# Two state-space convolutions, gated: Dskip added out of PSUM, the spilled tile stored and loaded by units, one tile for a chunk's last sum, u spectra stored in pairs, a new order of work

## The chip, the cores and the metric

The kernel runs on one core of a Trainium2 chip. A core has five engines, each with its own queue, which it works off in order: TensorE (PE in the profile; PEld is its loading of weights), VectorE (DVE), ScalarE (ACT), GpSimd (POOL) and SyncE (SP). SP here only issues transfers; 16 DMA engines carry them out. TensorE writes its sums to PSUM, the other tiles lie in SBUF. The metric is the device time of one execution in microseconds (us). Lower is better. The number given for the kernel is the median of three runs.

## The reference, cut to what matters

There are two parameter sets, A and B, over the same input u, with L = 2048 positions, D = 512 channels and N = 128 states. Each set makes a causal convolution kernel K for every channel out of 128 decaying, turning exponentials, convolves u with it by a Fourier transform of twice the length, and adds u times Dskip. A gate per position mixes the two results.

```python
def ref(u, A_re, A_im, B_re, B_im, C_re, C_im, log_dt, Dskip):
    dt = jnp.exp(log_dt)[:, None]
    logdA, dB = dt * (A_re + 1j * A_im), dt * (B_re + 1j * B_im)
    P = jnp.exp(logdA[:, :, None] * jnp.arange(L)[None, None, :])
    K = jnp.einsum("dn,dnl,dn->dl", C_re + 1j * C_im, P, dB).real
    Kf, Uf = rfft(pad(K, L)), rfft(pad(u.T, L))
    return irfft(Uf * Kf)[:, :L].T + u * Dskip

g = sigmoid((u * gate_w).sum(-1, keepdims=True))
out = g * ref(u, *A) + (1 - g) * ref(u, *B)
```

All data are float32. Adding Dskip to K at position 0 is the same as adding u times Dskip, and that is how both versions of the kernel do it.

## The kernel before, in words

The 512 channels are worked in NCH = 8 chunks of 64; with the two parameter sets a chunk has CH = 128 rows. A chunk is made of 8 tiles of 16 rows, 64 tiles T in all.

- `tables(T)` makes the exponentials of a tile as products of small tables. GpSimd makes angles (`ang`) and magnitudes (`mr`, "any": GpSimd or VectorE), ScalarE takes two sines and a square (L284), VectorE multiplies (`ei` and `mr`, L271 and L281). `kgen` (L588) sums over the 128 states on TensorE into a PSUM bank `c` and leaves the 16 rows of K. A copy of 256 columns (on ScalarE, L294, or VectorE, L296) brings them to half of an SBUF tile `kt` (L592). After each second tile VectorE adds Dskip (`dsk`) to column 0 of the eight groups in `kt` (L594), and `first` (L606) does the first step of the Fourier transform into `xa` or `xb`, the chunks in turn.
- `u_spectra` does the same for u, once for each pair of chunks b. Its eight spectra (L620) go from PSUM through a tile `z` to DRAM (`us`), 256 KB each. `gated` (L650) computes the gate into `gsi`, and loads its input through tiles `f`.
- `conv(c, j)` loads a spectrum of u back (`u<-us`), makes the spectrum of K (L620) and multiplies the two on VectorE (`y`, L684). After each second j, `back(c, U)` runs the first step of the inverse transform for unit U of four (`inv`, L704, 128 matmuls). Its two halves x are copied to a tile `z` each, and each is stored to the spilled tile `zb` of the chunk in DRAM, 256 KB (L712). In DRAM the half's four groups are rows 16x + 4U of 32; each row of `zb` has 136 x 128 places, of which 128 x 128 are used.
- `fin(cs, k)` does the last sum, for a quarter k of the positions. It loads 4 KB for each of 128 partitions from `zb` (512 KB a chunk, `f<-zb`), runs 32 matmuls (L740) with the gated weights `gsi`, copies the result to `o` and stores it. The chunks are taken in the groups FINS: three pairs, where one matmul spans two chunks (128 columns), then chunk 6 and chunk 7 alone (64 columns). A quarter needs all four units of its chunks. Chunk 7's four quarters are loaded in four pieces each: 192 KB, 192 KB, 64 KB and 64 KB, into tiles `ei` and `mr` that are free by then.

The order of all this is written out by hand. The body of `ssm_mix` calls the pieces one after the other, and `Plan` numbers each operation (0 to 1874) and notes which tiles it reads and writes. ORDER is a list of these numbers in the order in which they are emitted. So it sets the order within each engine's queue; a "b" behind a number takes the second of the engines that the operation allows (for a copy VectorE in place of ScalarE, for an "any" product VectorE in place of GpSimd, for a late store GpSimd's queue in place of SP's). `Plan.order` hands out the buffers of a ring (`z` 3, `f` 2, `o` 2, PSUM `c` 4) in that order, and an operation that takes a buffer waits for the users of the one before. All other transfers are issued by SP, in order: a transfer at the head of SP's queue that waits for its data holds up those behind it.

Of the kernel before, what the change touches and what calls it, by code (L numbers as in the profile page):

```python
# [34 lines left out]
FINS = ((0, 1), (2, 3), (4, 5), (6,), (7,))  # L35
# [11 lines left out]
def constants():  # L47
# [16 lines left out]
    si = np.stack([np.cos(ang).T, -np.sin(ang).T], 1).reshape(2 * G1, NB)  # L64
# [19 lines left out]
8 10 11 9 12 7 6 2 4 0 1 186 3 83 182 5 82 491 85 87 367 84 86 18 19 20 21 22 23 25 26 27 28 29 30 24 31 32 33 34 17 88 35 37  # L84
38 36 39 40 45 44 41 42 46 47 48 49 51 50 183 73 74 52 53 75 184 382 76 43 79 54 56 55 57 185b 58 187 61 189 62 188 138 67 59
60 63 64 65 68 69 70 71 72 369 66 77 370 371 78 372 81 384 383 80 385 91 92 93 94 95 190 194 342 96 16 13 98 99 101 100 191
102 104 89 373 103 105 192b 90b 376 195 374 375 377 401 107 196 106 193 386 378 379 108 109 402 380 197 387 388 15 14 127 219
# [3 lines left out]
133 131 445 199 425 368 437 438 439 440 441 208 448 226 212 200 1419 209 1430 449 446 426 447b 427 442 450 451 141 148 452  # L91
462 474 476 475 477 464 497 429 465 428 466 149 144 453 142 143 151 454 145 146 150 139 455 492 467 495 152 154 468 153 494
156 155 469 140 157 456 493 496 470 498 501 147 502 159 471 158 160 472 503 499 517 478 479 480 481 482 161 162 483 457 484
473 165 166 171 506 485 172 173 164 486 487 163 167 507 508 458 174 168 169 459 460b 175 500 177 179 504 625 628 627 626 629
170 505 488 518 515 516 532 533 534 344 490b 489b 509 510 1423 1420 1431 176 624 180 511 1424 1421 512 1432 1425 519 345 520
# [3 lines left out]
1446 559 1453 574 353 598 575 599 1447 1448 607 609 608 610 585 586 1454 601 354 1438 602 587 588b 355 589 560 1450 600 611  # L99
562 612 603 604 633 1466 613 761 649 356 561b 614 615 616 630 631 634 605 617 606b 650 357 1456 618 1457 635 636 637 619b 638  # L100
590 223 639 592 224 640 620 647 648 641 642 591b 225b 651 643 652 665 667 666 1440 1449 1451 234 227 621 653 229 228 644 623b
655 656 654 622 669 1458 1459 230 757 235 657 1461b 658 231 670 236b 237b 1463 1460 1474 1462 262 266 233b 232b 645 671 256
678 668 679 695 358 257 247 659 250 672 673 674 248b 675 680 696 681 682 646 251 683 660 359 363 685 686 241 253 1475 676 258
249 242 254 697 684 677 700 252 1771 255 243 661 361 365 698 1467 709 699 360 710 364 711 244 259 701 245 260 238 1464 687
1468 1476 688 239b 1465 689 703 690b 662 664b 704 691 1478 760 758 702 762 663 705 706 246 1485 1477 261 1469 1486 1776 240
1479 1487 707 712 726 728 727 366 362 713 1472 714 1470 708 716 717 715 692 739 729 740 718 719 1499 1488 1480 693 694 741
1481 730 1489 742 1490 720 1518 1471 766 1482 1473 1496 731 721 722 1500 723 1483 732 733 734 763 767 743 764 724 725 744
1491 735 1501 736 1497 1494b 1492b 737 747 1498 738b 263 267 265b 748 745 893 759 746 264 269 1484 1510 1493 1507 270 1502
769 768 780 765 770 781 771 749 750 268b 1503b 1505b 774 772 751 752 773 753 775 782 783 797 271 754 272 273 776 755b 756 799
784 785 777 800 787 274 1495 1504 1506 302 889 798 275 801 778 788 779b 277 276 786 284 1519 278 299 802 803 789 285b 790  # L110
1520 805 1777 1772 286 891 300 279 804 1511 1508 290 806 1512 1509 807 1773 791 811 812 813 291 815 1774b 808 1529 306 280
1521 1778 828 814 830 829 831 818 816 792 819 1779 817 296 297 843 832 281 1775 301 1781 292 809 833 810 282 820 793 821 841
835 822 293 287 283 842 844 836 834 823 824 845 874 859 837 838 1532 1782 294 846 847 848 892 890 894 794 288b 796b 795b 839
849 850 851 852 840b 1522 1513 860 861 872 873 862 875 1523 1530 853 295 1786 289 1514b 1516b 1531 854b 855 1787 1515 825 863
864 856 865 826 827 858 895 899 896 900 866 867 868 857b 869 876 877 879 1533 1524 1788 1534 880 878 1525 1789 901 298 1780
1540 1783 1527 904 870 905 881 1784b 871b 1544 1535 898 1543 1526 902 882 1545 1528 1551 883 1541 1025 906 1026 1023 1024 913
915 897 916 903 914 932 930 933 931 1536b 884b 1538b 1542 907 303 307 304 308 908 305b 309b 909 917 1562 1537 314 1539 1554
315 918 317 316b 910 885 1546 1547 919 920 886 921 1549b 943 887 888 934 911 922 923 944 963 310 311 1555 912 935 312 936 313
937 938 1517 1548 1552 924 318 1556 1553 948 949 945 319 925b 939 946 1563 330 336 327 940 1564 961 1030 962 964 947 1785
1550 1790 1796 320 1022 1791 1027 926 951 952 941 337 950 328 942 338 329 965 324 333 339 953 331b 332 954 325b 966 955 321  # L120
326 1565 967 956 334 340 993 322 968 969 976 974 977 975 970 927 978 929 979 957 971 991 994 992 972 928b 981 982 958 980 973
959 996 960 997 983 995 1007 1005 1008 1006 335 341 1576 1031 1573 984 999 1566 1557 1560 998 1558 1577 985 1574 1000 1567
1009 986 1010 1001 1012 1002 1568 323 1559 1575 1578 1013 1569b 1587 1584 1585 1003 1561 1570 1598 1156 1571 1011 1157 1004
1579 1588 1028 1034 1029 1032 1033 1045 1046 1035 1065 1014 1586 1015 1582b 1036 1016 1580 1037 1017 1047 1038 1606 1572 1581
1589 1590 1039 1040 987 1018 1048 1063 1049 1066 1064 1041 988 1050 1591 1593 1051 1042 1053 1052 990 989 1019 1043 1054 1592
# [76 lines left out]
def ssm_mix(ctx: ExitStack, tc: tile.TileContext, a, out, dry=False):  # L202
# [39 lines left out]
    if not dry:  # L242
# [13 lines left out]
        for b in range(NCH // 2):  # L256
            for j in range(NJ):
                tiles["uspec", b, j] = dp.tile([2, 128, 4 * DC], F32, name=f"us{b}_{j}")
# [575 lines left out]
```

## Time and profile before

| | us |
|---|---|
| median of 3 runs | 494.34 |
| lowest and highest | 491.32, 497.35 |
| the profiled execution, whole time | 495.32 |
| its span in the profile | 493.6 |

| transfer in the profile | count | KB each |
|---|---|---|
| zb<-z (store of half a unit) | 64 | 256 |
| f<-zb (load of a quarter) | 28 | 512 |
| mr<-zb, ei<-zb (chunk 7) | 8 and 8 | 192 and 64 |
| us<-z (a spectrum of u) | 32 | 256 |
| u<-us, with those into ml and mh | 64 | 256 |
| out_dram<-o | 12 and 8 | 256 and 128 |

How to read it: the span runs from the first to the last instruction; the rest of the execution's time lies around it. A row of groups gives line, engine, operation, the tiles (written <- read), the shape and the count, then busy us and the mean ns of one, then the idle time just before with what ended it. A row of the chain of what ended last gives the start in us, the length, and what ran. A row by stretches gives for each engine the busy us and the number of instructions, then the TensorE clock that was granted as a share, the share of time in which the DMA engines were busy, and what they moved in GB/s.

### The profile page before, as it was taken

The numbers are of one execution on the slowest core, as the hardware profiler recorded it, in microseconds if no ns is written. First come the engines' busy times: TensorE is split into PE (matmuls) and PEld (weight loads), VectorE is DVE, ScalarE is ACT, GpSimd is POOL, SyncE is SP. The second block draws the span as 40 slices with busy tenths as digits, with TensorE's granted clock in tenths as the row PEclk, the third lists the DMA queues.
The fourth block names the chain that finished last, engine by engine and source line by source line (L and its number), as shares of the span: only waits on it lengthen the run. The fifth ranks groups of instructions, "written<-read, shape, count | busy, mean of one in ns | idle before, by whom it ended". The sixth has DMA issues, their size and how long they took to land.

```text
span 493.6 us, 24249 instructions
## 1 busy us (share of the span) xinstructions
PE 375.8 (76%) x10768; PEld 337.1 (68%) x10768; DVE 424.4 (86%) x542; ACT 396.0 (80%) x673; POOL 332.1 (67%) x285
## 2 busy tenths in 40 slices
PE   3876726978869886798877888689888576989905
PEld 3765625867668775787867777678777466878805
DVE  6899999999989998789996999999999999874400
ACT  5988998977898988889897999999999777761210
POOL 4696882889775997489576697879677997600010
PEclk9987965999999999799998999899999979898967
DMA  6635751767055656367554655656567538263774
GB/s 196 234 113 179 215 167 34 238 227 218 5 148 184 196 165 187 111 193 246 157 171 123 194 159 158 189 174 201 164 179 221 176 108 281 87 194 112 196 222 139
DMA packets 78104, 84.66 MB, mean 172 GB/s; under 512 B 6064, under 2 KB 60720, under 8 KB 78000
## 3 DMA queue, kind: packets, MB, share of 16 engines
q1 hardware_dynamic: 77808, 82.59, 55.4%
q8 instruction: 84, 1.38, 1.1%
q0 software_dynamic: 192, 0.52, 0.3%
q14 instruction: 20, 0.16, 0.1%
HBM read 51.44 MB, written 31.65 MB: 168 GB/s over the span
## 4 chain that ended last, share of the span: by engine, by line
PE 34%; DVE 20%; ACT 16%; issue 14%; DMA 9%; POOL 5%; SPq 1%; DVEq 0%; ACTq 0%; POOLq 0%
PE c L620 9%; PE c L588 7%; PE c L704 5%; PE c L606 5%; DVE mr L281 5%; PE c L740 5%; DVE ei L271 4%; ACT s L284 4%; ACT ang L284 3%; DVE y L684 3%; ACT z L294 2%; DMA us<-z 2%; DMA zb<-z 2%; ACT sq L284 2%; POOL mr L271 2%
## 5 line engine op out<-in xcount | busy, mean ns | idle before, releaser
L281 DVE SCALAR_TENSOR_TENSOR mr<-sq,mr 128x1024 f32<-128x1024 f32 (+1 forms) x128 | 118.1, 948 | 3.8 <-ACT sq L284 3.8
L271 POOL TENSOR_TENSOR ang<-par,cint 128x512 int32<-128x512 int32 x64 | 67.1, 1049 | 66.1 <-ACT sq L284 52.8
L588 PE MATMUL c<-mr 128*32 128x64 f32 x2048 | 70.4, 232 | 50.6 <-DVE mr L281 27.9
L588 PEld LDWEIGHTS c<-mr 128*32 128x32 f32 x2048 | 53.3, 116 | 61.2 <-issue 25.5
L271 POOL TENSOR_TENSOR mr<-ml 128x1024 f32<-128x1024 f32 x43 | 84.2, 1958 | 15.5 <-PE c L588 12.1
L271 DVE TENSOR_TENSOR ei<-s,mr 128x1024 f32<-128x1024 f32 x64 | 77.8, 1216 | 5.5 <-PE c L588 2.7
L684 DVE TENSOR_TENSOR y<-c,u 128x1024 f32<-128x1024 f32 x57 | 68.7, 1216 | 9.4 <-PE c L620 9.1
L588 PE MATMUL c<-ei 128*32 128x64 f32 x2048 | 69.9, 229 | 3.4 <-issue 3.4
L284 ACT ACTIVATE s<-ang 128x1024 f32<-128x1024 int32 x64 | 66.0, 1031 | 5.1 <-DVE ei L281 3.9
L704 PE MATMUL c<-y,vv 64*64 64x128 f32 x1792 | 63.3, 281 | 7.3 <-DVE y L684 1.9
L284 ACT ACTIVATE ang<-ang 128x1024 f32<-128x1024 int32 x64 | 67.6, 1056 | 1.0
L271 POOL TENSOR_TENSOR ang<-sa 128x512 int32<-128x512 int32 x64 | 68.2, 1066 | 0.2
L284 ACT ACTIVATE sq<-ang 128x1024 f32<-128x1024 f32 x64 | 66.4, 1038 | 2.3 <-DVE mr L281 1.2
L271 POOL TENSOR_TENSOR mr<-mh 128x512 f32<-128x512 f32 x62 | 65.7, 1067 | 0.2
L704 PEld LDWEIGHTS c<-y,vv 64*64 64x64 f32 x1792 | 53.4, 138 | 13.5 <-DVE y L684 2.7
L588 PEld LDWEIGHTS c<-ei 128*32 128x32 f32 x2048 | 55.2, 117 | 4.0 <-issue 3.9
L620 PE MATMUL c<-xa,w 128*128 128x128 f32 x384 | 52.2, 286 | 4.7 <-DVE xa L296 2.0
L620 PE MATMUL c<-xb,w 128*128 128x128 f32 x384 | 54.5, 295 | 1.6 <-DVE xb L296 0.9
L606 PE MATMUL c<-small,kt 64*64 64x64 f32 x2048 | 43.9, 231 | 15.1 <-DVE kt L271 5.1
L294 ACT ACTIVATE z<-c 128x512 f32<-128x512 f32 x67 | 38.7, 595 | 17.7 <-PE c L704 8.7
L620 PEld LDWEIGHTS c<-xb,w 128*128 128x128 f32 x384 | 48.7, 203 | 5.8 <-issue 2.2
L606 PEld LDWEIGHTS c<-small,kt 64*64 64x64 f32 x2048 | 38.5, 143 | 20.5 <-issue 9.0
(109 smaller groups left out, 662.0 us busy)
## 6 DMA issues: line engine op xcount, KB each, us to landing
zb<-z SPq DMA_DIRECT2D x64, 256.0 KB
u<-us SPq DMA_DIRECT2D x57, 256.0 KB
f<-zb SPq DMA_DIRECT2D x28, 512.0 KB
us<-z SPq DMA_DIRECT2D x32, 256.0 KB
uin<-in_uk_dram SPq DMA_DIRECT2D x16, 256.0 KB
f<-in_ut_dram SPq DMA_DIRECT2D x8, 512.0 KB
out_dram<-o SPq DMA_DIRECT2D x12, 256.0 KB
par<-prd SPq DMA_DIRECT2D x7, 320.0 KB
```

Of the source, the lines that this page charges most:

```text
L271: lambda e: (dve if e == "dve" else pool).tensor_tensor(out=out(), in0=in0(), in1=in1(), op=o),
L281: lambda _: dve.scalar_tensor_tensor(out=out(), in0=in0(), scalar=s, in1=in1(), op0=o0, op1=o1), reads, writes, port=port)
L284: op("act", "act", n, lambda _: act.activation(out=out(), in_=in_(), func=func, **{k: v() if callable(v) else v for k, v in kw.items()}), ...
L294: act.activation(out=o(), in_=i(), func=AF.Copy)
L588: pe.matmul(ps[32 * j:32 * j + 32, o], x[:, 4 * o + j, 64:96], x[:, 4 * o + j, 0:64], start=part == 0, stop=part == 1, tile_position=(0, 3 ...
L606: pe.matmul(t(*ps[h])[64 * r:64 * r + 64, 64 * g:64 * g + 64], t(*x)[64 * h:64 * h + 64, g], t("small")[64 * h:64 * h + 64, 64 * r:64 * r ...
L620: pe.matmul(view()[:, :, k], t("w2", j // 2)[:, 4 * (j % 2) + k], t(*x1)[:, 4 * j + k], start=True, stop=True)
L684: op("dve", "tt1", 1024, lambda _: dve.tensor_tensor(out=t(*y).rearrange("p h s f d -> p h s (f d)"), in0=fv().rearrange("p s f d -> p s ( ...
L704: pe.matmul(bank_of(x)[64 * e:64 * e + 64, CH * q:CH * q + CH], v[:, 0:64] if h else v[:, 32:96], t(*ys[f // 4])[64 * x:64 * x + 64, h, :, ...
L740: pe.matmul(t(*ps)[64 * r:64 * r + 64, m * DC * i:m * DC * i + m * DC].rearrange("p (c d) -> p c d", c=m), t("gsi")[:, 4 * k + i, s, 64 * ...
```

## The change

- *Dskip.* The copy of K's rows leaves column 0 out (252 columns for 256), and VectorE writes column 0 of every tile as a sum of the PSUM bank and `dsk`: 64 additions of 4 columns for 32 of 8.
- *The spilled tile.* `zb` has rows of 128 x 128, numbered 8U + 4x, so that a unit lies in one piece of DRAM. A tile `z` holds both halves of a unit, and one transfer of 512 KB stores it. As soon as it is stored it is loaded, 512 KB, to partitions 32U to 32U + 31 of a tile that holds the whole chunk, one row of 16 KB for each partition. Only the last unit of chunk 7 goes in two stores and two loads. The gate weights' rows (`si`) are reordered to fit.
- *One tile for the last sum.* `f` is one tile of a whole chunk (128 x 32 x 128), which the gate's input shares; chunk 7 takes the place of `xa`. `fin` runs for each chunk alone: 8 x 4 blocks of 32 matmuls of 64 columns, with outputs of 128 KB, for 12 blocks of 128 columns and 8 of 64.
- *u spectra.* Two of them share a tile `z` and are stored with one transfer of 512 KB.
- *Rings.* `z` 2 tiles of 4 KB a partition for 3 of 2 KB; `f` 1 of 16 KB for 2 of 8 KB; `o` 2 of 1 KB for 2 of 2 KB.
- *Order.* ORDER is a new list of 1885 numbers. `Plan` gets a list `touch`, for operations that use a tile's buffer whose data they wait for under a finer key.

```diff
-FINS = ((0, 1), (2, 3), (4, 5), (6,), (7,))
...
-    si = np.stack([np.cos(ang).T, -np.sin(ang).T], 1).reshape(2 * G1, NB)
+    si = np.stack([np.cos(ang).T, -np.sin(ang).T], 1).reshape(2, 4, 16, NB).transpose(1, 0, 2, 3).reshape(2 * G1, NB)
...
 ORDER = """
-8 10 11 9 12 7 6 2 4 0 1 186 3 83 182 5 82 491 85 87 367 84 86 18 19 20 21 22 23 25 26 27 28 29 30 24 31 32 33 34 17 88 35 37
...
+2 4 0 182 1 83 3 479 5 82 84 86 85 15 351 87 186 13 16 8 10 6 11 7 18 19 20 21 22 23 25 26 24 27 28 29 30 31 32 33 34 35 37
...
-    def __call__(self, engs, kind, n, fn, reads=(), writes=(), table=None, port=False):
+    def __call__(self, engs, kind, n, fn, reads=(), writes=(), table=None, port=False, touch=()):
         i = len(self.ops)
-        deps, new = set(), []
+        deps, after, new = set(), set(), []
+        for k in touch:
+            after.update(self.writers[k][:1])
+            self.users[k].append(i)
...
-    ring("z", 3, [128, 4, CH])
-    ring("f", 2, [128, 2, 8, CH])
-    ring("o", 2, [128, 2, 4, DC])
+    ring("z", 2, [128, 2, 4, CH])
+    ring("f", 1, [128, NA, CH])
+    ring("o", 2, [128, 4, DC])
...
-    ring("zb", 8, [32, 136, CH], F32, DRAM)
+    ring("zb", 8, [32, 128, CH], F32, DRAM)
...
-        copy(256, lambda: t(*kt)[:, 4 * (T % 2):4 * (T % 2) + 4], lambda: t(*kc)[:, 0:256].rearrange("p (o l) -> p o l", o=4), [kc], [kt])
+        kv = lambda x, lo, hi: x.rearrange("p (o l) -> p o l", o=4)[:, :, lo:hi]
+        ko = lambda lo, hi: t(*kt)[:, 4 * (T % 2):4 * (T % 2) + 4, lo:hi]
+        copy(252, lambda: ko(1, 64), lambda: kv(t(*kc)[:, 0:256], 1, 64), [kc], [kt])
+        tt("dve", 4, lambda: ko(0, 1), lambda: kv(t(*kc)[:, 0:256], 0, 1), lambda: t("dsk", c)[:, g].unsqueeze(2), OP.add,
+           [kc, ("dsk", c)], [kt], port=False)
         if T % 2:
-            tt("dve", 8, lambda: t(*kt)[:, :, 0], lambda: t(*kt)[:, :, 0],
-               lambda: t("dsk", c)[:, g - 1:g + 1].rearrange("p t o -> p (t o)"), OP.add, [kt, ("dsk", c)], [kt])
             first(("k", T), kt, (("xa", "xb")[c % 2], c), G * (g - 1))
...
-            dma(256, lambda j=j: t("uspec", b, j).rearrange("h p x -> p h x"),
-                lambda zv=zv: zv().rearrange("p (h x) -> p h x", h=2), [z], [("uspec", b, j)])
+            if j % 2:
+                dma(512, lambda j=j: t("uspec", b, j // 2).rearrange("h p x -> p h x"),
+                    lambda z=z: t(*z).rearrange("p j f c -> p (j f c)").rearrange("p (h x) -> p h x", h=4), [z],
+                    [("uspec", b, j // 2)])
...
-            copy(512, lambda z=z: t(*z).rearrange("p q k -> p (q k)"), lambda x=x: bank_of(x), [ps[0 if last else x]], [z])
-            dma(256, lambda x=x: t(*zb)[16 * x + 4 * U:16 * x + 4 * U + 4, 0:128].rearrange("g p k -> p g k"), lambda z=z: t(*z),
-                [z], [zb, ("zbu", c, U)])
+            copy(512, lambda x=x: t(*z)[:, x].rearrange("p q k -> p (q k)"), lambda x=x: bank_of(x), [ps[0 if last else x]],
+                 [z] * (x == 0) + [("zx", c, U, x)], [z] * x)
+        for xs in ((0,), (1,)) if end else ((0, 1),):
+            g, n = 8 * U + 4 * xs[0], 4 * len(xs)
+            dma(128 * n // 2, lambda g=g, n=n: t(*zb)[g:g + n].rearrange("g p k -> p g k"),
+                lambda xs=xs: t(*z)[:, xs[0]:xs[-1] + 1].rearrange("p x q k -> p (x q) k"),
+                [("zx", c, U, x) for x in xs], [zb] * (U == 0) + [("zu", c, U)], touch=[z] + [zb] * (U > 0))
+        for h in range(1 + end):
+            m = NA // (1 + end)
+            dma(16 * m, lambda h=h, m=m: t(*f)[32 * U:32 * U + 32, m * h:m * h + m],
+                lambda h=h, m=m: t(*zb)[8 * U:8 * U + 8].rearrange("g (m a) k -> (g m) a k", m=4)[:, m * h:m * h + m],
+                [("zu", c, U)], [f] * (U == 0) + [("fu", c, U, h)], touch=[zb] + [f] * (U > 0))
+
+    def home(c):
+        return ("f", c) if c < NCH - 1 else ("xa", "fin")
...
-                        pe.matmul(t(*ps)[64 * r:64 * r + 64, m * DC * i:m * DC * i + m * DC].rearrange("p (c d) -> p c d", c=m),
-                                  t("gsi")[:, 4 * k + i, s, 64 * r:64 * r + 64],
-                                  fv()[:, :, 2 * i + r, DC * s:DC * s + DC], start=s == 0, stop=s == 1, tile_position=(0, 64 * r))
+                        pe.matmul(t(*ps)[64 * r:64 * r + 64, DC * i:DC * i + DC], t("gsi")[:, 4 * k + i, s, 64 * r:64 * r + 64],
+                                  t(*f)[:, 8 * k + 2 * i + r, DC * s:DC * s + DC], start=s == 0, stop=s == 1, tile_position=(0, 64 * r))
...
-    for cs in FINS:
+    for c in range(NCH):
         for k in range(4):
-            fin(cs, k)
+            fin(c, k)
```

More of the change, by code (lines that the diff above doesn't have):

```diff
@@ L91 @@
[L91 to L94, printed above, removed]
@@ L102 @@
[L102 to L105, printed above, removed]
@@ L256, in ssm_mix @@
         for b in range(NCH // 2):
-            for j in range(NJ):
-                tiles["uspec", b, j] = dp.tile([2, 128, 4 * DC], F32, name=f"us{b}_{j}")
+            for j in range(NJ // 2):
+                tiles["uspec", b, j] = dp.tile([4, 128, 4 * DC], F32, name=f"us{b}_{j}")
         ctx.enter_context(tc.manual_schedule())
```

169 lines of the change are left out of this document (83 added, 86 removed), and 27 rows, old and new, of the table ORDER.

## The prediction, made before the changed kernel was run

> **What bounds the kernel now.** I read the page of the profile first: busy times, slices, the chain that ended last, the groups by line. The next question was whether one limit holds over the whole span, so I asked for three stretches: to 420 us, from there to the end of the last inverse matmul (468.78 us), and the rest.
>
> ```profile
> span 493.6 us, 24249 instructions
> PE 375.8 (76%) x10768; PEld 337.1 (68%) x10768; DVE 424.4 (86%) x542; ACT 396.0 (80%) x673; POOL 332.1 (67%) x285
> q8 instruction: 84, 1.38, 1.1%
> PE 34%; DVE 20%; ACT 16%; issue 14%; DMA 9%; POOL 5%; SPq 1%; DVEq 0%; ACTq 0%; POOLq 0%
> ```
> ```profile
> core 0: us, PE busy (x) PEld busy (x) DVE busy (x) ACT busy (x) POOL busy (x), PEclk, DMA share, GB/s
> 0.00:420.00 420.00, 323.01 (x9392) 288.34 (x9392) 392.67 (x507) 370.42 (x631) 320.59 (x273) 0.94 0.57 174
> 420.00:468.78 48.78, 44.51 (x1186) 40.96 (x1188) 30.22 (x33) 23.16 (x36) 9.13 (x8) 0.93 0.52 149
> 468.78:493.60 24.82, 8.24 (x192) 7.77 (x192) 1.54 (x3) 2.41 (x6) 2.33 (x4) 0.71 0.61 180
> ```
>
> There are three kernels in one. To 420 us VectorE is busy 392.67 of 420 us (93%), ScalarE 88%, TensorE 77%: VectorE binds, but the chain gives it only 20% of the steps, so work hops between engines that are all nearly full. From 420 to 468.78 TensorE binds (44.51 of 48.78 us). The last 24.82 us bind on nobody: no engine is busy a third of it. They are a round trip through DRAM, and the chain shows it:
>
> ```profile
> 466.77 2.01 PE sq L704 x64
> ...
> 468.86 0.70 DVE z L296
> ...
> 472.77 5.26 DMA zb<-z
> ...
> 478.10 3.34 DMA ei<-zb
> ...
> 481.69 1.99 PE c L740 x32
> ...
> 490.47 0.38 ACT o L294
> ```
> ```profile
> 469.58 0.38 SPq L289 DMA_DIRECT2D zb<-z  x1
> 470.13 1.80 SPq L289 DMA_DIRECT2D mr<-zb  x2
> 471.98 0.76 SPq L289 DMA_DIRECT2D ei<-zb  x1
> 472.77 0.51 SPq L289 DMA_DIRECT2D zb<-z  x1
> ...
> 473.88 4.85 SPq L289 DMA_DIRECT2D ei<-zb  x4
> ...
> 484.61 1.45 SPq L289 DMA_DIRECT2D ei<-zb  x2
> ```
>
> The last store issues at 472.77, 3.21 us after the copy at 468.86 ended (469.56): three loads of chunk 7 stand ahead of it on SP's queue.
>
> **The change, part by part.** The sum is made against this execution: 495.32 us, that is the span of 493.6 and 1.7 around it; the median of the runs is 494.34, 0.98 lower.
>
> ```profile
> L271 DVE TENSOR_TENSOR kt<-kt,dsk x32: 161/336/2082, 41.1 to 445.2; 128x8 f32<-128x8 f32 x32
> ```
> ```profile
> L684 DVE TENSOR_TENSOR y<-c,u x57: 1207/1216/1225, 90.4 to 464.3; 128x1024 f32<-128x1024 f32 x57
> ...
>   DMA u<-us: 0.2, 1
> ```
> ```profile
> L271 DVE TENSOR_TENSOR kt<-kt,dsk 128x8 f32<-128x8 f32 x32 | 17.7, 556 | 1.0 <-ACT kt L294 0.6
> ...
> L296 DVE COPY z<-c 128x512 f32<-128x512 f32 x21 | 14.1, 683 | 1.8 <-PE c L620 1.2 <-PE c L704 0.5
> L294 ACT ACTIVATE o<-c 128x512 f32<-128x512 f32 (+1 forms) x15 | 7.7, 514 | 27.3 <-DMA out_dram<-o 18.6 <-PE c L740 8.6
> L296 DVE COPY kt<-c 128x256 f32<-128x256 f32 x18 | 7.5, 418 | 4.8 <-PE c L588 4.7
> ...
> L271 DVE TENSOR_TENSOR mr<-mh 128x512 f32<-128x512 f32 x2 | 2.3, 1153 | 0.0
> ```
>
> 1. *Dskip.* 32 additions of 8 columns with both inputs in SBUF go; 64 of 4 columns come, one input in PSUM. The old ones take 161 ns at best, 556 in the mean, 2082 at worst, 17.7 us in all: eight columns are not work of 2 us, so they are held up by something. The y products, one input in PSUM, never spread (1207 to 1225 ns). So I take the new ones as not held: copies from PSUM cost 418 ns for 256 columns and 683 for 512, 153 ns plus 1.035 a column, and four columns come to 157 ns. 64 x 0.16 = 10.2 us, 7.5 less than before. The other end is the old mean, 64 x 0.556 = 35.6 us, or 17.9 more; the spread of y speaks against it. The copy beside it shrinks from 256 to 252 columns: nothing. VectorE binds to 420 us, but is idle 27 us of it; I take four fifths of the 7.5, that is -6.0 (0 to -7.5). What the new adds put on VectorE's queue is a wait for the matmul of L588 at each tile: behind it stand the table products that everything needs. Priced below.
>
> 2. *Who copies.* Counting the calls in the order of the body numbers the operations, so the new list tells each one's engine (a "b" takes the second choice). VectorE gets 3 more kt copies (+1.25), 9 copies to o of 256 columns for 3 of 512 and 2 of 256 (+0.9), one z or us copy less (-0.7), two gate copies (+1.4), one mr product less (-1.15): +1.7 us. ScalarE's count changes under 1 us in all. Same weight: +1.4 (0 to +1.7).
>
> 3. *The last sums.* Three pairs of chunks were summed at 128 columns a matmul; now each chunk has 32 x 4 of 64 columns.
>
> ```profile
> 423.67 4.02 PE c L740 x64
> ...
> 460.15 1.08 PE c L740 x32
> ```
>
> A block of 32 costs 2.01 us at 128 columns and 1.08 at 64 (the second is chunk 6's). Before: 12 x 2.01 + 8 x 1.08 = 32.8; after: 32 x 1.08 = 34.6, so +1.8 us and 384 more matmuls, each with its weight load. TensorE has 34% of the chain: +0.6 (0 to +1.8).
>
> 4. *Instructions.* TensorE idles on "issue", on nothing that the profile shows, in the middle of blocks of matmuls:
>
> ```profile
> PEld c L588 <- issue: 29.4, 39, 3.4
> ```
> ```profile
> 261.05 0.85 PE L606 MATMUL c<-small,uin 64*64 64x64 f32 x41
> 264.05 0.92 PE L606 MATMUL c<-small,uin 64*64 64x64 f32 x23 [2.15 <-issue]
> ```
>
> The block at 264.05 had run 41 of its 64 matmuls when it stopped. The queue of kind "instruction" moved 84 packets, 1.38 MB for 24,249 instructions, 57 bytes each, so I read such stops as late instructions; that is an inference. 768 more make 44 KB, 2.7 packets more; with 29.4 us over 84 packets at 0.35 us each: +0.9 (0 to +3).
>
> 5. *Transfers.* Stores to zb fall from 64 to 33, loads from 44 to 33, us stores from 32 to 16; stores to the output grow from 20 to 32: SP and POOL issue 114 for 160, at 0.4 to 0.5 us each some 20 us of queue. SPq is 1% of the chain: 0 (-2 to 0). The new list puts a unit's load one or two places behind its own store on SP in 7 of 33 cases, where SP stands 4 to 5 us until the store has landed (5.26 above), with loads of u behind it. VectorE now waits 0.2 us in all for u, and most u loads are issued some tens of steps before their product: 0 (to +4). Two tiles z of twice the size for three: a tile is held for two copies and one store; 0 (-3 to +3). One tile f for two: a chunk's first load waits for the four last sums of the chunk before, and the list has all four ahead of it; 0. On TensorE at least 10.6 us of work lies between a chunk's last inverse and its first sum (chunks 0 to 6, by the durations of these rows), enough for 0.7 + 5.3 + 3.3. Each load now fills 32 partitions with rows of 16 KB where it filled 128 with rows of 4 KB: 0 in the sum, the first rival. zb loses its padding rows: no row prices it, 0.
>
> 6. *The end.* Chunk 7's units are loaded as they come; behind the last inverse the queue has three stores, then a load of unit 1, one output, unit 2, then the last unit in halves. The last store issues at about +1.6 us from the inverse's end (0.7 copy, two issues) where it was +4.0: -2.4. Store and load stay 5.26 and 3.34, though a load of 512 KB stands ahead now (+1.5 to 2.4). From the first sum (481.69) to the end is 11.9 us now, since two of the last quarter's loads are issued only at 484.61; after, both halves are there together: four blocks of at most 1.99, a copy, and the 3.1 us after the last copy, some 9.5 with an output wait, -2.4; together -2.4 + 1.9 - 2.4 = -2.9. Eight further loads of chunk 7 no longer stand in the queue and on the rings in between: -1.5. And one block of chunk 6's sums (1.08) moves behind the last inverse, where TensorE is idle. The end: -5.5 (-10 to +3).
>
> 7. *The new order.* Nothing in the trace of before prices it. Its idle time of VectorE to 420 us is 27 us; a third either way is 0 (-9 to +9).
>
> Sum: -6.0 + 1.4 + 0.6 + 0.9 - 5.5 = -8.6; 495.3 - 8.6 = 486.7 for a profiled execution, **486 us** against the median.
>
> **Rivals.** *A, slower: loads into 32 partitions hold the rings.* Two stretches of the end are both filled with loads and stores at the same share of DMA time, at very different rates:
>
> ```profile
> 472.00:474.00 2.00, 0.00 (x0) 0.00 (x0) 0.00 (x0) 0.00 (x0) 0.00 (x0) 0.55 0.98 348
> 474.00:476.00 2.00, 0.00 (x0) 0.00 (x0) 0.00 (x0) 0.00 (x0) 0.00 (x0) 0.50 0.97 215
> ```
>
> In both, chunk 7's loads into 48 and 16 partitions run (those of 473.88 among them) beside other traffic; what makes the second slow the trace does not say, so the pair is an outer bound. At 348 GB/s 512 KB take 1.51 us, at 215 GB/s 2.44; 33 loads hold the engines 31 us longer, and everything behind them (u, instructions) comes later. Where half of that lands on the path, +15.5: 501 us; it decides once 8.6 of the 31 do. Against it: the DMA share is 0.57 before 420 us, and VectorE waits 0.2 us for u.
>
> [...]
>
> *B, no change: VectorE's gain turns into waits.* With TensorE and "issue" at 48% of the chain, a shorter VectorE may only wait more. Then 1 and 2 are worth 0, and the end half: 495.3 + 1.5 - 2.8 = 494.0, 493 against the median.
>
> *C, slower: the adds wait for TensorE.* 18 kt copies waited 4.7 us for L588, 0.26 each. If the 64 adds do too, that is 16.7 us, and a wait of the engine that binds counts whole: 495.3 - 8.6 + 16.7 = 503.4, 502 against the median. It decides above 8.6 / 64 = 0.13 us an add. Against it: the list places half of the adds 4.0 us or more of VectorE's work behind the last product that their matmul needs, as it did before.
>
> **How the numbers follow.** The forecast has 0.53, B 0.25, A 0.13, C 0.09. About 1% is what a measurement of this kernel can tell from no change: under 489.4 is faster, over 499.3 slower. The low ends of the forecast's terms add up to some 23 us; they will hardly all fall one way, so I take 15 down, and 9 up, beyond which it is a rival: 471 to 495 is the forecast's own range. So a little of it is no change (0.04), as a little of B is faster (0.02). Faster 0.51, same 0.27, slower 0.22. The range, 471 to 502, leaves out 0.1 above and somewhat less below.
>
> **What would show it.** VectorE's adds at 0.15 to 0.2 us each, 10 us in all; its busy time some 6 us down; the last sums at L740's successor near 35 us; the stretch from the last inverse to the end at 19 to 20 us for 24.82; more idle time on "issue" by 1 us. I am wrong by A if u or the loads into f appear as waits of VectorE or TensorE, or the DMA share rises above 0.65; by B if VectorE's idle time before its last table product grows by what its busy time loses; by C if the adds wait for the matmul; and by the order if VectorE's idle time changes by more than 9 us with none of these.

## The result: 3% slower, where 2% faster was forecast

| | before | after |
|---|---|---|
| median of 4 runs, us | 495.11 | 509.51 |
| lowest and highest | 491.32, 497.35 | 507.08, 512.45 |
| profiled execution, whole time and span | 495.32, 493.6 | 512.45, 510.7 |

The ratio is 1.030, with a 95% interval of 1.021 to 1.039. The time lies above the forecast's range (471 to 502). Some executions of a kernel fall in a slower state; all ratios here leave those out, the medians do not.

From the page of the kernel after: the span, the busy times, the transfer queues, the chain by engine.

```profile
span 510.7 us, 24915 instructions
PE 392.7 (77%) x11152; PEld 349.4 (68%) x11152; DVE 418.6 (82%) x581; ACT 396.5 (78%) x677; POOL 332.7 (65%) x283
q1 hardware_dynamic: 74592, 82.98, 56.9%
q8 instruction: 87, 1.43, 1.2%
PE 42%; DVE 22%; ACT 15%; issue 13%; DMA 4%; POOL 3%; SPq 0%; DVEq 0%; ACTq 0%; POOLq 0%
```

VectorE is busy 5.8 us less (424.4 to 418.6), as worked out. But the span grew by 17.1, so VectorE idles 23 us more, and TensorE's part of the chain rose from 34% to 42%. TensorE is also busy 16.9 us longer (375.8 to 392.7). The rows of its last sums make 2.2 of that (35.8 to 38.0); the rest lies in rows that the change leaves as they were, and no run explains it. The next rows are groups and waits of the kernel after (a wait: us in all, times, longest).

```profile
L272 DVE TENSOR_TENSOR kt<-c,dsk 128x4 f32<-128x4 f32 x64 | 10.1, 160 | 26.6 <-ACT kt L295 21.3 <-PE c L589 5.2
```
```profile
DVE kt L272 <- ACT kt L295: 21.3, 20, 3.9
...
PE c L589 <- issue: 13.3, 13, 3.1
PE c L609 <- issue: 12.2, 11, 3.1
PE c L710 <- issue: 11.0, 9, 2.6
...
PE c L742 <- issue: 4.3, 4, 1.7
```

The adds take 0.16 us each, 10.1 in all, which is term 1 to a tenth. They also wait 26.6 us, 21.3 of it until ScalarE's copy out of the same bank has ended. And TensorE stands on "issue", on nothing that the profile shows: 41.2 us in 38 places (40.8 in these four rows), where before it was 18.8 us in 20 places, with these two rows as the largest:

```profile
PE c L588 <- issue: 10.7, 10, 2.2
...
PE c L606 <- issue: 5.8, 6, 2.1
```

The transfers of the kernel after (count, KB each, median us from issue to landing), and the end of its chain:

```profile
zb<-z SPq DMA_DIRECT2D x31, 512.0 KB, 4.3
...
f<-zb SPq DMA_DIRECT2D x28, 512.0 KB, 5.6
us<-z SPq DMA_DIRECT2D x16, 512.0 KB, 3.8
...
xa<-zb SPq DMA_DIRECT2D x3, 512.0 KB, 6.6
```
```profile
486.74 1.95 PE sq L710 x64
490.12 3.06 DMA zb<-z
493.56 7.55 DMA xa<-zb
501.27 6.13 PE c L742 x128
```

A load of a unit into `f` takes 1.3 to 1.8 us longer to land than a store of the same size (5.6 for 4.3 and 3.8). From the last inverse (488.69) to the end are 22.0 us, for 24.8 before: 2.8 of the 5.5 us of term 6; the last load takes 7.55 us, where 3.34 stood in the sum. VectorE's last table product begins at 460.0, for 440.8 before. So the loss is made ahead of the end.

```profile
L281 DVE SCALAR_TENSOR_TENSOR mr<-sq,mr x128: 673/949/1226, 26.8 to 440.8; 128x1024 f32<-128x1024 f32 x64, 128x512 f32<-128x512 f32 x64
```
```profile
L282 DVE SCALAR_TENSOR_TENSOR mr<-sq,mr x128: 675/946/1226, 30.8 to 460.0; 128x1024 f32<-128x1024 f32 x64, 128x512 f32<-128x512 f32 x64
```

### The profile page after: what moved, and what is told of

Its sections match the earlier page's. It is cut to its first block, busy times and chain, and to the rows that moved or that the text cites. A ratio compares the mean times of both kernels' runs of the same rounds, so it can differ in the third digit from the quotient of the medians.

```text
span 510.7 us, 24915 instructions
## 1 busy us (share of the span) xinstructions
PE 392.7 (77%) x11152; PEld 349.4 (68%) x11152; DVE 418.6 (82%) x581; ACT 396.5 (78%) x677; POOL 332.7 (65%) x283
## 2 busy tenths in 40 slices
DMA packets 74746, 84.69 MB, mean 166 GB/s; under 512 B 5456, under 2 KB 60496, under 8 KB 73584
## 3 DMA queue, kind: packets, MB, share of 16 engines
q1 hardware_dynamic: 74592, 82.98, 56.9%
q8 instruction: 87, 1.43, 1.2%
## 4 chain that ended last, share of the span: by engine, by line
PE 42%; DVE 22%; ACT 15%; issue 13%; DMA 4%; POOL 3%; SPq 0%; DVEq 0%; ACTq 0%; POOLq 0%
PE c L623 11%; PE c L589 8%; PE c L710 8%; PE c L609 7%; PE c L742 6%; DVE mr L282 5%; DVE ei L272 4%; DVE y L690 4%; ACT s L285 2%; ACT sq L285 2%; ACT ang L285 2%; ACT L285 2%; DMA xa<-zb 1%; DVE mr L272 1%; ACT z L295 1%
## 5 line engine op out<-in xcount | busy, mean ns | idle before, releaser
L589 PE MATMUL c<-mr 128*32 128x64 f32 x2048 | 72.8, 235 | 26.3 <-issue 7.4
L589 PEld LDWEIGHTS c<-mr 128*32 128x32 f32 x2048 | 53.8, 118 | 37.4 <-issue 28.5
L710 PE MATMUL c<-y,vv 64*64 64x128 f32 x1792 | 66.2, 285 | 16.1 <-issue 11.0
L589 PE MATMUL c<-ei 128*32 128x64 f32 x2048 | 72.4, 233 | 6.0 <-issue 5.9
L710 PEld LDWEIGHTS c<-y,vv 64*64 64x64 f32 x1792 | 55.4, 140 | 22.6 <-issue 13.7
L272 POOL TENSOR_TENSOR mr<-mh 128x512 f32<-128x512 f32 x63 | 67.2, 1072 | 4.1 <-PE c L589 3.9
L589 PEld LDWEIGHTS c<-ei 128*32 128x32 f32 x2048 | 56.3, 119 | 6.3 <-issue 6.2
L623 PE MATMUL c<-xb,w 128*128 128x128 f32 x384 | 55.0, 297 | 5.6 <-ACT xb L295 3.0
L623 PE MATMUL c<-xa,w 128*128 128x128 f32 x384 | 53.2, 288 | 6.9 <-ACT z L295 3.5
L295 ACT ACTIVATE z<-c 128x512 f32<-128x512 f32 x70 | 39.9, 592 | 21.5 <-PE c L710 17.6
L623 PEld LDWEIGHTS c<-xb,w 128*128 128x128 f32 x384 | 49.1, 205 | 9.9 <-ACT xb L295 3.2
L623 PEld LDWEIGHTS c<-xa,w 128*128 128x128 f32 x384 | 47.2, 197 | 11.0 <-ACT z L295 4.1
```

The lines of the kernel that those rows point to most:

```text
L272: lambda e: (dve if e == "dve" else pool).tensor_tensor(out=out(), in0=in0(), in1=in1(), op=o),
L295: act.activation(out=o(), in_=i(), func=AF.Copy)
L589: pe.matmul(ps[32 * j:32 * j + 32, o], x[:, 4 * o + j, 64:96], x[:, 4 * o + j, 0:64], start=part == 0, stop=part == 1, tile_position=(0, 3 ...
L623: pe.matmul(view()[:, :, k], t("w2", j // 2)[:, 4 * (j % 2) + k], t(*x1)[:, 4 * j + k], start=True, stop=True)
L710: pe.matmul(bank_of(x)[64 * e:64 * e + 64, CH * q:CH * q + CH], v[:, 0:64] if h else v[:, 32:96], t(*ys[f // 4])[64 * x:64 * x + 64, h, :, ...
```

## The experiments

Ratios are to the kernel before, run beside each on the same chip. "Issue" is TensorE's idle time on issue in the profiled execution, "landing" the median for the loads into f where the trace gives one. Issue is no price by itself: kernels that are slow for another reason (v5_later, v14_split, v12_oldorder) stop less than the kernel after.

| run | median us | ratio, 95% interval | landing, us | issue, us |
|---|---|---|---|---|
| after | 509.51 | 1.030, 1.021 to 1.039 | 5.6 | 41.2 |
| v1_aside | 515.27 | 1.038, 1.030 to 1.046 | 5.7 | 38.4 |
| v2_paired | 510.54 | 1.033, 1.025 to 1.041 | 5.7 | 38.9 |
| v3_load128 | 499.65 | 1.004, 0.999 to 1.010 | 5.0 | 31.9 |
| v5_later | 535.11 | 1.071, 1.060 to 1.082 | 5.6 | 22.1 |
| v10_spread | 501.15 | 1.012, 1.004 to 1.021 | 4.5 | 33.2 |
| v7_cut4 | 512.35 | 1.034, 1.027 to 1.042 | 5.6 | 46.3 |
| v6_paired128 | 502.71 | 1.012, 1.003 to 1.021 | 4.7 | 33.6 |
| v16_wide | 491.59 | 0.991, 0.987 to 0.995 | 4.8 | 23.4 |
| v23_widepaired | 495.16 | 1.002, 0.998 to 1.006 | 4.8 | 23.3 |
| b17_narrow | 504.94 | 1.018, 1.011 to 1.025 | - | 22.8 |
| b1_adds | 519.73 | 1.050, 1.044 to 1.055 | - | 28.1 |
| b20_end | 500.77 | 1.011, 1.006 to 1.016 | 5.3 | 16.4 |
| b3_end | 507.87 | 1.024, 1.020 to 1.029 | 4.8 | 22.7 |
| b3b_end | 505.47 | 1.021, 1.014 to 1.028 | 6.9 | 16.9 |
| v14_split | 536.41 | 1.075, 1.064 to 1.086 | 4.6 | 19.5 |
| v13_padded | 522.06 | 1.052, 1.046 to 1.058 | - | 42.4 |
| v8_quarters | 513.14 | 1.033, 1.024 to 1.042 | 6.9 | 39.1 |
| v12_oldorder | 607.61 | 1.230, 1.220 to 1.239 | 4.4 | 21.5 |

### Do the adds' waits cost the time?

v1_aside writes the sums to a tile of their own, which nobody reads (Dskip is left out); v2_paired adds Dskip as before the change, in the new order; v5_later moves the adds behind up to four more of VectorE's instructions.

```diff
-        tt("dve", 4, lambda: ko(0, 1), ...
+        tt("dve", 4, lambda: t("aside").unsqueeze(2), ...
```


> The changed kernel, but the 64 additions write to a tile of their own and the copies take all 256 columns, so Dskip is left out of the output. All instructions, their order and the reads of PSUM stay; only the common tile kt of copy and addition is gone. Theory K (each addition waits for ScalarE's copy into the same tile kt, and VectorE loses that time, 21.3 us in 20 waits): these waits go to under 3 us and the time falls to 490 to 498 us. Theory O (the new order is worse as a whole, the waits of the additions only show it): the waits go elsewhere on VectorE and the time stays at 504 to 511. Theory L (loads into 32 partitions hold the DMA rings and delay instructions): 507 to 511. If ScalarE and VectorE wait for each other because both read one PSUM bank, the waits stay as they are.

> The changed kernel with the Dskip part undone: copies of 256 columns, and 32 additions of 8 columns with both inputs in SBUF, each behind the two copies of its pair; the order is otherwise the new one. Theory K: VectorE gets some 7 us of busy time back but loses most of the 26 us of waits at the additions, so 492 to 501 us. Theory O: 505 to 514. Theory L: 507 to 512.

> The changed kernel with one thing moved: each addition stands up to four VectorE instructions later in the order (193 places in all for 64 additions), where buffers allow it. Theory K: the waits of the additions fall from 26.5 us to under 8 and the time to 494 to 502; a PSUM bank is held longer, which may cost TensorE up to 5 us of that. Theory O: the same wait turns up elsewhere, 505 to 511. Theory L: 507 to 511.

The waits of v1_aside stay, so they are not for the common tile kt; what the add and the copy still share is the bank. In the trace the add waits for a semaphore that the copy sets, so the program as built puts the two in turn; that the chip itself would is not shown.

```profile
DVE aside L272 <- ACT kt L295: 22.0, 19, 4.0
```

In v2_paired the wait for ScalarE falls to 7.9 us, and the time stays (510.54). But its 32 old adds take longer themselves:

```profile
L270 DVE TENSOR_TENSOR kt<-kt,dsk 128x8 f32<-128x8 f32 x32 | 21.7, 677 | 8.5 <-ACT kt L293 7.9
```

Work and waits together the adds cost VectorE 30.2 us there, for 36.7 in the kernel after and 18.7 before. So undoing the Dskip part gains nothing in the kernel as changed; what the waits alone cost, no run here separates. In v5_later only 2.5 us of waiting is left, and the kernel is 4% (20 us) slower than after: VectorE's y products wait 35.1 us for L623, for 11.9 after, which fits banks that are held longer.

### Are the loads slow because they fill few partitions?

v3_load128 spreads each unit's 512 KB over 128 partitions, 4 KB each (the data are mixed up). v10_spread is the clean form: the same 32 rows of 16 KB, into every fourth partition, with the gate weights' rows put in the same order. v7_cut4 keeps 32 adjacent partitions and cuts the rows into pieces of 4 KB (data mixed up).

```diff
-            dma(16 * m, lambda h=h, m=m: t(*f)[32 * U:32 * U + 32, m * h:m * h + m],
+            dma(16 * m, lambda h=h, m=m: t(*f)[U:128:4, m * h:m * h + m],
```


> The changed kernel, but each load of a unit goes to 128 partitions with 4 KB each for 32 partitions with 16 KB each; the bytes land in other places, so the last sums are of mixed data. Theory L: a load lands in 3.5 to 4.5 us for 5.6, TensorE's idle time on issue falls by more than 10 us, and the time falls to 495 to 503. Theory K or O: the loads land sooner, but outside the end nothing waits for them, so 505 to 510.

> The changed kernel, but a unit's 32 rows of 16 KB land in every fourth partition (U, U+4, ..., U+124) in place of 32 adjacent ones; the rows of the gate weights are put in the same order, so the result is whole. Theory L (few adjacent partitions are slow to fill): loads into f land in about 5.0 us for 5.6, PE's idle time on issue falls from 41 to about 32 us, time about 500 us (496 to 503). Rival R (long rows of 16 KB are what holds the rings): as the changed kernel, 5.6 us, 41 us, 507 to 513 us.

> The changed kernel, but each unit's load into its 32 adjacent partitions is cut into 128 pieces of 4 KB (four for each partition, data mixed, so the output is not the reference's). Theory L: nothing changes, 507 to 513 us, loads into f land in 5.6 us. Rival R (long rows): about 500 us and 5.0 us.

Transfers of v10_spread, then the same row of v7_cut4:

```profile
f<-zb SPq DMA_DIRECT2D x28, 512.0 KB, 4.5
...
xa<-zb SPq DMA_DIRECT2D x3, 512.0 KB, 5.6
```
```profile
f<-zb SPq DMA_DIRECT2D x28, 512.0 KB, 5.6
```

It is the partitions, not the length of the rows. In the packet records a 16 KB packet of these loads takes 1.082 us in the mean into adjacent partitions, 0.824 into every fourth (992 packets each); the 4 KB pieces of these loads take 0.28 us in v7_cut4 and 0.20 in v3_load128. So a packet into adjacent partitions takes 1.3 to 1.4 times as long in the mean, and one of 16 KB 1.7 times in the median (1.116 against 0.644 us). What in the chip makes it so, no run shows.

The signs that rival A named do not come: hardly any engine waits for u or for f (TensorE 0.5 us for f in the kernel after). What changes is "issue", 41.2 to 33.2 us, and it changes around the loads: stops that end between a load's issue and 2 us after its landing make 21.3 us in the kernel after and 10.4 in v10_spread (24.0 in v7_cut4, 12.9 in v3_load128), all others 19.9 and 22.7 (22.4 and 19.0). Spreading the rows is worth 1.8% (9 us), and between the runs with 4 KB pieces 3.0% (15 us). v10_spread also shows the end as forecast. Its chain:

```profile
477.44 2.01 PE sq L710 x64
...
480.91 3.11 DMA zb<-z
...
484.54 4.66 DMA xa<-zb
...
489.22 6.10 PE c L742 x128
```

From 479.45 to the span's end at 498.6 are 19.15 us, 5.7 less than before.

### What is left: late instructions, and the narrow last sums

The order of TensorE's records says where it stops. Numbering all of them from the start (weight loads, matmuls and the waits of its queue) and counting a matmul with its weight load, the stops on issue of the kernel after begin at

```
2753 3009 3521 5057 6081 6849 7617 7873 9409 9665 9921 10177 10689 10945 11201 ...
```

36 of the 38, and 19 of the 20 before, leave the remainder 193 when divided by 256. The timeline of TensorE in the kernel after shows one such stretch (start us, us, line, count, idle before):

```profile
308.85 1.15 PE L742 MATMUL c<-f,gsi 128*64 128x64 f32 x32
309.93 0.92 PE L609 MATMUL c<-small,kt 64*64 64x64 f32 x44
311.94 0.51 PE L609 MATMUL c<-small,kt 64*64 64x64 f32 x19 [1.10 <-issue]
312.24 0.32 PE L710 MATMUL c<-y,vv 64*64 64x128 f32 x2
312.29 0.22 PE L609 MATMUL c<-small,kt 64*64 64x64 f32 x1
312.35 0.32 PE L710 MATMUL c<-y,vv 64*64 64x128 f32 x2
313.29 1.96 PE L710 MATMUL c<-y,vv 64*64 64x128 f32 x60 [0.62 <-DVE xa L297]
315.19 1.16 PE L623 MATMUL c<-xb,w 128*128 128x128 f32 x8
316.28 0.80 PE L609 MATMUL c<-small,kt 64*64 64x64 f32 x36
317.32 0.68 PE L609 MATMUL c<-small,kt 64*64 64x64 f32 x28 [0.24 <-issue]
```

Between the stops at 311.94 and 317.32 lie 19 + 2 + 1 + 2 + 60 + 8 + 36 = 128 matmuls, with their weight loads 256 instructions. The instruction queue moved 87 packets of 1.43 MB in all, 16.4 KB each, that is 64 bytes for each of 256 instructions.

So I read a stop as the next group of 256 not there yet, and the packet records bear it out. Behind the first 193, TensorE's 22,444 records need 87 groups, and its 21,680 before need 84, just the packets that the queue moved (so the 57 bytes in step 4 of the prediction, over all engines' instructions, misread the queue). Each of the 36 stops ends 1.2 to 1.8 us after the packet of its group has landed, each of the 19 before 1.2 to 1.6.

The stops go with how fast a group is used up against how long the next takes to come: in the kernel after, groups ahead of a stop were used up in 3.9 us in the median, and the next packet landed 3.7 us in the mean after their start; for the others it is 5.3 and 2.6. The last sums of 64 columns use 64 instructions in 1.08 us, those of 128 columns in 2.01: 17 of the 38 stops come within 8 us after a last sum, in stretches that make up 28% of the span, and none of the 20 before (22%). That is a hint only; two runs test it.

v16_wide makes each block of last sums of 16 matmuls of 128 columns (two positions share a weight), b17_narrow gives the kernel before the narrow sums. v14_split stores v10_spread's units in halves again, the first as soon as it is copied.

```diff
-            for i in range(4):
+            for i in range(0, 4, 2):
...
-                        pe.matmul(t(*ps)[64 * r:64 * r + 64, DC * i:DC * i + DC], ...
+                        pe.matmul(t(*ps)[64 * r:64 * r + 64, DC * i:DC * i + 2 * DC].rearrange("p (c d) -> p c d", c=2), ...
```


> The kernel with loads to every fourth partition (501.15), with the last sums as 16 matmuls of 128 columns for each block of 32 of 64: the same columns, half the instructions (two positions share one weight, so the output is not the reference's). Theory I (TensorE stops at the ends of groups of 256 of its instructions, since blocks of 64 columns use instructions up at twice the rate): TensorE's idle time on issue falls from 33 to 20 to 26 us, and the time to 490 to 497 us. Rival (their number and rate do not matter): 498 to 504 us, 30 to 36 us on issue.

> The kernel before, with its paired last sums as matmuls of 64 columns, one chunk at a time (384 matmuls more; the result is whole). Terms 3 and 4 of the prediction alone: +1.5, that is 496 to 498 us. Theory I: TensorE's idle time on issue rises from 18.8 to 23 to 30 us, and the time to 498 to 505 us. Where the old order has slack enough: 494 to 496 us.

> The kernel with loads to every fourth partition (501.15), with each unit stored in two halves again, 256 KB each, the first as soon as its copy is done (32 stores more). Theory J (stores of 512 KB hold the rings ahead of the instructions): idle time on issue under 27 us and 491 to 498 us. Rival (the size of a store does not matter): 498 to 505 us, 30 to 36 us on issue.

The groups of last sums, first of v10_spread, then of v16_wide (busy us, mean ns, idle before), and the last table product of v16_wide:

```profile
L742 PE MATMUL c<-f,gsi 128*64 128x64 f32 x896 | 32.1, 229 | 6.8 <-issue 4.4 <-ACT xa L295 1.2 <-ACT z L295 0.8
```
```profile
L742 PE MATMUL c<-f,gsi 128*64 128x128 f32 x448 | 31.1, 288 | 3.3 <-ACT z L295 1.5 <-issue 0.7 <-DVE y L690 0.5
```
```profile
L282 DVE SCALAR_TENSOR_TENSOR mr<-sq,mr x128: 671/944/1225, 30.5 to 443.5; 128x1024 f32<-128x1024 f32 x64, 128x512 f32<-128x512 f32 x64
```

The same columns in half the instructions give 2.1% (10 us), with 9.8 us less on issue. That is 512 matmuls fewer, where the change added 384: v16_wide also widens chunks 6 and 7, which were narrow before. In the old order the narrow sums cost 1.8% (9 us), with 4.0 us more on issue and 2.9 more of TensorE's work: there I can lay only about 7 of the 9 us to them by the trace. v14_split came out at 536.41 (1.075, 1.064 to 1.086), with 19.5 us on issue but VectorE's y products 9.0 us behind u: the new stores stand ahead of u's loads on SP's queue and wait for copies (SP waits 141.2 us for ScalarE's copies to z, for 63.9 in v10_spread). It tells nothing on the size of a store, which stays open.

### Are the adds worth anything once these two are out of the way?

v6_paired128 undoes the Dskip part beside quick loads (data mixed up), v23_widepaired in v16_wide. b1_adds puts it alone into the kernel before, each add right behind its copy or up to three of VectorE's instructions later.

> Loads of units to 128 partitions of 4 KB each (data mixed) and, on top, Dskip added once for two tiles in SBUF as before the change. If the 20 us that the adds wait for ScalarE's read of the bank count once the loads are quick (theory K2): 490 to 496 us. If they are hidden with quick loads too: 497 to 502 us, as with quick loads alone (499.65).

> The kernel with loads to every fourth partition and last sums of 128 columns (491.59), with Dskip added once for two tiles in SBUF as before the change. If the adds out of PSUM are worth the forecast's term 1 (-6.0): 495 to 499 us. If the waits eat it (rival B of the prediction): 490 to 494 us. If they cost more than they save: 484 to 489 us.

> The kernel before with the Dskip part alone: 64 additions of 4 columns out of PSUM for 32 of 8 in SBUF, half of them later than their copy by two or three of VectorE's operations. Term 1 of the prediction: -6.0, that is 488 to 491 us. If the adds wait for the copy's read of the same bank as they do after the change (20 us in all) and the waits eat the gain: 494 to 498 us. If they cost more than they save: over 499 us.

v6_paired128 can't be told from v3_load128. But v23_widepaired is 1.1% (5 us) slower than v16_wide, and the intervals don't meet: there the Dskip part is worth nearly the 6.0 us of term 1. Its old adds:

```profile
L270 DVE TENSOR_TENSOR kt<-kt,dsk 128x8 f32<-128x8 f32 x32 | 26.0, 814 | 7.0 <-ACT kt L293 6.6
```

In the old order, at the places that I gave them, the same adds cost 25 us. Two waits stand out there:

```profile
PE c L588 <- DVE kt L271: 14.8, 7, 6.8
...
DVE kt L271 <- ACT kt L294: 14.1, 12, 2.8
```

In the program as built a bank is free only when the add has run too, so I read its place in VectorE's order as what decides; v5_later, which moves nothing but these places, speaks for it.

### The end alone, and other arrangements

b3_end, b3b_end and b20_end give the kernel before chunk 7's loads by half units of 256 KB, each into 16 adjacent partitions as it comes. In b3_end a copy waits for an output that I had put behind the loads (507.87); b3b_end mends that (505.47); b20_end takes the padding of zb away too and puts the last stores first. The load of b20_end:

```diff
+            dma(256, lambda g=g: t("xa", "fin")[4 * g:4 * g + 16].rearrange("p a k -> p (a k)"),
+                lambda g=g: t(*zb)[g:g + 4].rearrange("g (m a) k -> (g m) (a k)", m=4), [("zbu", c, U, x)], [("xa", "fin")])
```


> The kernel before with chunk 7 alone loaded as it comes: each half unit, 256 KB, into 16 adjacent partitions with rows of 16 KB, for 16 loads of 192 and 64 KB. Term 6 of the prediction for the loads (-5.5 less the chunk 6 block of 1.1): 489 to 492 us, and 20.5 to 22 us from the last inverse's end to the end of the span, for 24.8. If few partitions slow these loads as after the change: 492 to 496 us and 22 to 25 us.

> The kernel before, with chunk 7 alone loaded as it comes, as in b3_end, but with the output of chunk 6's quarter 1 ahead of these loads on SP's queue, so that no copy waits for it. Term 6 of the prediction: 489 to 492 us, 20.5 to 22.5 us from the last inverse's end to the end of the span, for 24.8. If few adjacent partitions slow these loads too: 492 to 496 us.

> The kernel before, with zb's rows without padding, so that the 16 rows of a half unit's load are of one stride, and chunk 7 loaded as it comes, half units of 256 KB into 16 adjacent partitions; the last unit's stores go ahead of the third unit's... loads on SP's queue, and chunk 6's last quarter goes ahead of chunk 7's first on TensorE. The result is whole. If the 19 us that the last loads took with padding were loads on 4 of 16 engines: they land in 4 to 6 us, and the end takes 19 to 21 us from the last inverse, for 24.8: 488 to 491 us. If loads into 16 adjacent partitions are slow in any case: 494 to 505 us.

Stretches of b3b_end, then of b20_end, in which hardly anything but these loads runs (the last three columns are the granted clock, the DMA share and GB/s):

```profile
480.00:488.00 8.00, 0.00 (x0) 0.00 (x0) 0.00 (x0) 0.00 (x0) 0.00 (x0) 0.50 0.25 107
```
```profile
472.00:482.00 10.00, 0.27 (x5) 0.08 (x2) 0.00 (x0) 0.38 (x1) 1.25 (x2) 0.50 0.90 136
```

With padding the rows are not merged, the load's first dimension is 4, and the DMA share of 0.25 is that of 4 of 16 engines at work. Without padding the first dimension is 16 and the share 0.90, at 136 GB/s, and the last loads, issued by 471.96, are used at 483.04. From the last inverse to the end are 38.1 us in b3b_end and 28.9 in b20_end, for 24.8 before. The smallest packets, taken as one for each engine that a transfer uses, fit the reading that the first dimension limits the engines: in the trace of the kernel after, q1's 4,032 packets of 4 bytes are 16 for each of its 252 transfers; before they are 4,592, that is 128 fewer than 16 for each of 295, and 128 are missing if chunk 7's 8 loads with a first dimension of 4 have 4 each and its 8 with 12 have 12. So I take the new end to need loads that are both merged and spread, as v10_spread has them (19.15 us); the layout of the kernel before doesn't give that.

v13_padded is v10_spread with the padding put back: 522.06 (1.052, 1.046 to 1.058). Its load has 8 rows by 4 pieces, and q1 moved 74,328 packets for 74,592, that is 264 fewer, all under 512 bytes (5,192 for 5,456), 8 for each of 33 loads. At one such packet for each engine, as above, I read that as 8 engines for 16, an estimate; issue rose to 42.4 us. The padding itself was so not tested.

> The kernel with loads to every fourth partition (501.15), with the padding of zb's rows in DRAM put back (136 x 128 places a row for 128 x 128). If the lost padding costs: 493 to 498 us and stores of 512 KB under the 4.3 us that they take now. If it costs nothing: 498 to 504 us and 4.3 us.

v8_quarters loads chunks 0 to 6 by quarters into all partitions, four loads in a row: 513.14 (1.033, 1.024 to 1.042), landing in 6.9 us, with 39.1 us on issue. So loads into all partitions are no cure when they come in a burst. v12_oldorder is v10_spread with the old order put back as far as it goes: 607.61 (1.230, 1.220 to 1.239). The pieces that are new had to be fitted in by hand, and VectorE's adds alone wait 33.3 us for ScalarE there; it shows how much such a list can lose, not what the new one is worth.

> The changed kernel, but chunks 0 to 6 are loaded by quarters again, four loads of 128 rows of 4 KB at the place of the chunk's last unit load; chunk 7 by units as in the change. Theory L: 498 to 504 us, with loads into f as quick as before the change; if the burst of 2 MB makes the last sums or the u loads wait, PE shows waits for f or VectorE for u, and 503 to 510 us.

> The kernel with loads to every fourth partition (501.15), with the order of work of the kernel before put back as far as the new pieces allow (the common operations keep their old engines and, on each engine, nearly their old order; joint stores stand where the second half's store stood, unit loads behind the next unit's store, last sums where the new order has them). Theory O (the new order costs what is left, against the 486 forecast): 487 to 494 us, VectorE's waits back near 27 us to 420 us. Rival (what is left is in the joint stores, the padding or the last sums, whatever the order): 498 to 504 us.

## Why the prediction was wrong, by its steps

- *Term 5, transfers: 0.* This failed first: "Each load now fills 32 partitions ...: 0 in the sum, the first rival". Adjacent partitions cost 9 to 15 us (v10_spread against after, v7_cut4 against v3_load128). Rival A named the cause, came near the size (15.5) and had instructions come later too, but its signs were waits for u or f, or a DMA share above 0.65. Neither came: the share of q1 rose from 55.4% to 56.9%. The price appears as instructions that come late to TensorE.
- *Terms 3 and 4, last sums and instructions: +1.5 together.* Mis-sized. I took TensorE's 1.8 us by its share of the chain, and three more packets at 0.35 us each, the mean over all packets. The runs show 9 us for the 384 matmuls in the old order (b17_narrow) and 10 us for 512 in the new one (v16_wide). A packet costs nothing or up to 3.1 us, by how dense the work around it is, and narrow matmuls nearly halve the time that a group lasts (64 instructions in 1.08 us for 2.01). The 1.08 us of a narrow block was right, but it is no measure of what the block does to the next one.
- *Term 1, Dskip: -6.0.* The adds' own time was right (10.1 us for 10.2). The step that failed is the wait ahead of them, priced for the matmul of L588 alone (rival C) and at nothing in the sum: with their waits the adds take 36.7 us of VectorE's time, for 18.7 before. As long as TensorE was late, undoing the part changed nothing (v2_paired), which fits rival B; with loads and sums mended it is worth 5 us (v23_widepaired). The waits are not rival C's (5.2 us for L589) but for ScalarE's copy out of the bank, 21.3 us, which I hadn't priced.
- *Term 6, the end: -5.5.* Right as a mechanism. It gave 2.8 us with the slow loads and 5.7 with the spread ones; the line that failed in it is "Store and load stay 5.26 and 3.34": they took 3.06 and 7.55.
- *Terms 2 and 7, moved copies and order: +1.4 and 0.* In v16_wide the last table product begins at 443.5, 2.7 us later than before, where terms 1 and 2 would make it 4.6 earlier. Some 7 us are so left to the order and all that was not tried alone, inside the bounds of 9 that I gave. What the new order is worth stays open. Each part that was put alone into the old order made it slower (b1_adds, b17_narrow, b3b_end, b20_end), so the prices read there hold for that order.

The miss is 23.5 us (509.5 for 486). Loads (9 or more), last sums (some 6 to 8 beyond the forecast) and the gain of term 1 that could not show (up to 6) make it up; they overlap, so I don't add them more closely. No whole version tried beats the kernel before: v16_wide does, by 0.9%, but shares weights between positions, and the quickest whole one with the change is v10_spread.

## What to carry to other kernels

Before a change makes a hot engine's instructions smaller and more numerous, look whether it already stops on nothing that the profile shows in the middle of blocks: price the density of instructions, not their count. When a load is reshaped, look at which partitions it fills (here 5.6 us to land in adjacent ones, 4.5 in every fourth) and at the size of its first dimension (a DMA share of 0.25 at 4, 0.90 at 16), and look for the price not only at whoever waits for the load: here TensorE waited 0.5 us for f ahead of the end, and stood on issue for 41.2 us, for 33.2 with the rows spread. And a gain on one engine can show only after the stalls of its neighbours are gone (of Dskip nothing in v2_paired, 5 us in v23_widepaired), so undo parts in the mended kernel, not only in the one that disappoints.

## What the runs showed of the hardware that was not expected

TensorE's instructions come in groups of 256 (87 packets for 22,444 records after, 84 for 21,680 before), and its unexplained stops lie at their ends: 19 of 20 before, 36 of 38 after, 21 of 24 in v16_wide. Each of these ends 1.2 to 1.8 us after a packet of 16 KB has landed on the instruction queue. The same 32 rows of 16 KB land in 4.5 us in every fourth partition and in 5.6 in adjacent ones. The program as built lets VectorE's add wait for ScalarE's copy out of one bank even where they share no tile to be written: 22.0 us in 19 places in v1_aside.
